# Two token blocks take turns over the halves of a layer's weights while those weights are still being split

## The chip, the core and the metric

The kernel runs on one core of a Trainium2 chip. Its engines are named as in the profile: PE (TensorE), DVE (VectorE), ACT (ScalarE), POOL (GpSimd) and SP (SyncE, which here only issues DMAs). The metric is the device time of one execution in microseconds. The kernel before takes 863.5 us (median of three runs, 862.19 to 864.65).

## What is computed

A linear attention with a decaying state, a two-layer network and a mixture of eight experts, all in float32:

```python
for t in range(S):                                   # B=4, H=8, S=768, D=48
    cur = einsum('bhd,bhe->bhde', u[None] * kt, vt)
    y[:, :, t] = einsum('bhd,bhde->bhe', rt, state + cur)
    state = wt[:, :, :, None] * state + einsum('bhd,bhe->bhde', kt, vt)
x = y as (3072, 384)
h = x @ w_in                                         # 384 -> 2048
x = (maximum(h, 0) + alpha * minimum(h, 0)) @ w_out  # 2048 -> 384
logits = x @ w_gate ; one expert of 8 for each token
out = gate * (maximum(x @ w1[e], 0) @ w2[e])
```

The part of `y` that comes from `u` is a diagonal term: for each token and head, c = sum over d of r*k*u, and then c*v.

## The kernel before

The 3072 tokens are 24 tiles of 128. Each tile goes through the attention (`att_tile`): a scan of the decays and its reciprocal on DVE (`scan`, `rec0`, `rec1`, `k`), r times the decays on POOL (`r`), scores on PE (`sc`), copied by ACT (`a0`, `a1`) and masked by POOL (`m0`, `m1`), the transposed k (`ktr` on PE, `ko` on ACT), the state (`kv`, `st`), the output on PE (`yst`, `yav0`, `yav1`), the sum with the diagonal term on DVE (`fin`), a transpose (`xtr`) and its split in a high and a low part (`xh` on ACT, `xl` on DVE). The diagonal term is made by two POOL products (`rk`: r*k, then *u), a sum over d on DVE (`c`) and a product with v (`cv`; on ACT for tiles 0 to 2, else on POOL).

Three tiles are a block of 384 tokens; there are eight. For each block the first layer pair runs in 16 steps, one for each 128 of the 2048 hidden columns. A step is nine matmuls of `p1` (three chunks of 384, each as high*high, high*low and low*high), an activation in three operations (ACT `gn`, DVE `gt`, then ACT `gh` and DVE `gl`, the split of the result) and, two steps later, nine matmuls of `p2` into three PSUM banks that hold the block's output. `p1` writes to two PSUM buffers and the splits have three, so PE can run some two steps ahead of DVE.

The weights arrive in 16 packed pieces, j = 0 to 15, even ones of w_in and odd ones of w_out. A piece is needed from hidden step j (an even j and the odd one behind it serve two steps). `wl_stages` unpacks each: ACT `rebase`, three operations of DVE (`words`), ACT `high`, and `low` on DVE for even j, on POOL for odd j. The raw words have two buffers, and so have the unpacked ones.

What sets the order: all steps are put into numbered slots, two for each step of PE; attention tiles, weight pieces and gates are hung on slots by the tables OPS, PRO_OPS and PRO_MOVED and by `s_tile`. Slots below zero are the prologue (tiles 0 to 2 and the first pieces) in a written order on all engines. From step 0 on the order on PE and POOL is as written, and a scheduler sets it on DVE, ACT and SP. Every engine works through its own list in order, so that an instruction that waits holds up all behind it.

When a block's 16 steps are done, `p2_out` copies its three banks into x2 (two by ACT, one by DVE), and `gate_block` makes the gate logits of the first six blocks on DVE: 24 products with a sum (`lv`, L492), four at a time over some 12 steps. After eight blocks follow the experts, in 16 units. `constants` (POOL, at the end of the prologue) makes index tables for the gates, and oma_s = 1 - alpha, which `gt` reads.

Of the kernel before, what the change touches and what calls it, by code (L numbers as in the profile page):

```python
# [99 lines left out]
def attention_mlp_moe(ctx, tc, dmaj, tmaj, ub, alpha, w_in, w_out, w_gate, w_gate_b, wexp, out):  # L100
# [23 lines left out]
    def load_tile(i):  # L124
        if i < NB:
# [11 lines left out]
        sp.dma_start(out=tm, in_=tmaj[i])  # L137
# [22 lines left out]
    ub_s = cst.tile([128, DM], F32, name="ub_s")  # L160
    al_s = cst.tile([128, NF1], F32, name="al_s")
# [106 lines left out]
    def att_tile(i, s0):  # L268
        cx = {}
        blk, j = divmod(i, NB)  # L270
        first, last = i % CPB == 0, i % CPB == CPB - 1
# [5 lines left out]
        def scan():  # L277
            dm = dm_t[i]
            ex = ap.tile([PR, NP, 129], F32, tag="ex", name="ex")
# [32 lines left out]
        def diag():  # L312
            tm = tm_t[i]
# [132 lines left out]
        def x_low():  # L446
# [162 lines left out]
    def p2(blk, f):  # L609
        if f == 0:  # L610
# [489 lines left out]
```

## Time and profile before

| | |
|---|---|
| median of the runs | 863.5 us |
| the profiled execution | 865.37 us, span 863.6 us, mean clock of PE 0.974 of full |
| busy over the span | PE 94%, DVE 74%, ACT 45%, POOL 35% |
| first matmul of step 0 (block 0) | 40.97 us |
| first of block 1, block 2, block 3 | 135.21, 202.73, 268.61 us |
| length of block 0, 1, 2 | 94.2, 67.5, 65.9 us |
| idle time of PE from 40 to 170 us that ended with something else's release | 23 us |

The starts of the blocks are found by counting the matmuls of L591 in the timeline of PE, nine for each step. The views used are: busy time by stretch, who waited for whom, groups of instructions by line and shape in a stretch, the DMA issues, and the timeline. Where durations of one engine overlap a little, an instruction begins some 0.08 us before the one ahead is recorded as ended.

### The profile page before, as it was taken

How to read it: one execution, taken by the hardware profiler on the slowest of the kernel's cores; microseconds unless marked ns; L12 is line 12 of the kernel's file. 1: busy time of each engine (PE TensorE's matmuls, PEld its weight loads, DVE VectorE, ACT ScalarE, POOL GpSimd, SP SyncE). 2: the span in 40 equal slices, each digit the busy share in tenths (PEclk: the TensorE clock that was granted, in tenths of full speed). 3: DMA queues.
4: the chain of work that ended last, by engine and by line, in shares of the span. 5: the costliest groups of instructions: out<-in, count | busy, mean ns of one | idle time of the engine just before them, and what ended most of it. 6: DMA issues, size and time to landing. Idle time of an engine off the chain costs nothing. (4 is left out here: it accounts for less than half of the span.)

```text
span 863.6 us, 14591 instructions
## 1 busy us (share of the span) xinstructions
PE 812.2 (94%) x5453; PEld 787.7 (91%) x5453; DVE 640.4 (74%) x1219; ACT 385.0 (45%) x751; POOL 298.4 (35%) x309
## 2 busy tenths in 40 slices
PE   6868779999999999999999999999899999999994
PEld 4767769999999999999999999989899999999993
DVE  6999997976967977976976973446766676767761
ACT  3555453343333334333334333346445566665641
POOL 5466654324433324334234341122423122322301
PEclk8788999999999999999999999999999999999998
DMA  9734543022324122322122300055367577686830
GB/s 277 213 107 149 200 147 122 29 60 87 60 60 117 32 60 66 83 60 84 63 61 60 88 1 1 28 201 211 120 235 250 195 237 282 228 288 194 287 104 21
DMA packets 30513, 111.59 MB, mean 129 GB/s; under 512 B 8229, under 2 KB 11592, under 8 KB 30440
## 3 DMA queue, kind: packets, MB, share of 16 engines
q1 hardware_dynamic: 26088, 100.38, 36.6%
q0 software_dynamic: 4352, 10.26, 3.3%
q8 instruction: 44, 0.72, 0.3%
q14 instruction: 29, 0.24, 0.1%
HBM read 100.95 MB, written 10.45 MB: 129 GB/s over the span
## 5 line engine op out<-in xcount | busy, mean ns | idle before, releaser
L591 PE MATMUL ph<-xth,wih 128*128 128x384 f32 x384 | 136.3, 355 | 11.1 <-DVE gt L596 9.0
L602 ACT CAST gh<-gt 128x384 fp32r<-128x384 f32 x128 | 65.6, 513 | 170.9 <-DVE gt L596 170.9
L617 PE MATMUL py<-woh,gh 128*128 128x384 f32 x384 | 136.6, 356 | 2.6 <-DVE x L628 1.3
L591 PE MATMUL ph<-xth,wil 128*128 128x384 f32 x384 | 131.0, 341 | 4.8 <-DVE wil L232 4.8
L591 PE MATMUL ph<-xtl,wih 128*128 128x384 f32 x384 | 130.9, 341 | 0.8 <-DVE xtl L449 0.8
L617 PE MATMUL py<-woh,gl 128*128 128x384 f32 x384 | 129.9, 338 | 0.0
L617 PE MATMUL py<-wol,gh 128*128 128x384 f32 x384 | 129.4, 337 | 0.0
L604 DVE TENSOR_TENSOR gl<-gt,gh 128x384 fp32r<-128x384 f32 x128 | 86.4, 675 | 32.9 <-ACT gh L602 31.3
L594 ACT ACTIVATE gn<-ph 128x384 f32<-128x384 f32 x128 | 62.5, 488 | 100.8 <-PE ph L591 97.1
L596 DVE SCALAR_TENSOR_TENSOR gt<-gn,oma_s,ph 128x384 f32<-128x384 f32 x128 | 76.4, 597 | 41.0 <-ACT gn L594 40.4
L492 DVE SCALAR_TENSOR_TENSOR sink<-x,wgb 128x384 f32<-128x384 f32 x144 | 98.8, 711 | 1.5 <-ACT x L628 1.2
L822 DVE SCALAR_TENSOR_TENSOR gl<-ph,gh 128x256 fp32r<-128x256 f32 x96 | 40.4, 422 | 74.0 <-ACT gh L820 73.7
L591 PEld LDWEIGHTS ph<-xth,wih 128*128 128x128 f32 x384 | 73.4, 191 | 13.2 <-DVE gt L596 9.9
L891 POOL DMA_INDIRECT out<-ys,meta x28 | 28.2, 1006 | 158.3 <-ACT ys L888 103.3
L817 PE MATMUL ph<-xh,w1h 128*128 128x256 f32 x288 | 81.1, 282 | 1.7 <-DVE gl L822 1.7
L817 PE MATMUL ph<-xh,w1l 128*128 128x256 f32 x288 | 80.8, 281 | 0.0
L817 PE MATMUL ph<-xl,w1h 128*128 128x256 f32 x288 | 80.3, 279 | 0.0
L591 PEld LDWEIGHTS ph<-xth,wil 128*128 128x128 f32 x384 | 73.2, 191 | 6.1 <-DVE wil L232 6.1
L617 PEld LDWEIGHTS py<-woh,gh 128*128 128x128 f32 x384 | 73.1, 190 | 5.2 <-DVE x L628 1.9
L363 POOL TENSOR_SCALAR_AFFINE_SELECT at<-at 128x512 f32<-128x512 f32 x46 | 37.2, 830 | 112.1 <-ACT at L359 112.1
L591 PEld LDWEIGHTS ph<-xtl,wih 128*128 128x128 f32 x384 | 73.5, 191 | 1.8 <-DVE xtl L449 1.6
L617 PEld LDWEIGHTS py<-woh,gl 128*128 128x128 f32 x384 | 72.8, 189 | 0.6 <-DVE gl L604 0.6
(211 smaller groups left out, 1939.2 us busy)
## 6 DMA issues: line engine op xcount, KB each, us to landing
raw<-w SPq DMA_DIRECT2D x64, 768.0 KB, 4.8
dm<-dmaj SPq DMA_DIRECT2D x21, 673.8 KB, 4.7
tm<-tmaj SPq DMA_DIRECT2D x21, 576.0 KB, 3.8
raw<-w_out SPq DMA_DIRECT2D x8, 768.0 KB, 4.4
raw<-w_in SPq DMA_DIRECT2D x7, 768.0 KB, 4.3
x2d<-x SPq DMA_DIRECT2D x8, 576.0 KB, 3.6
both<-tmaj SPq DMA_DIRECT2D x3, 576.0 KB, 9.1
wgb<-w_gate_b SPq DMA_DIRECT2D x2, 768.0 KB
```

What stands on the lines that cost most here:

```text
L363: pool.affine_select(out=cx[jj], in_=cx[jj], pattern=[[0, NP], [1, 128]], compare_op=ALU.is_gt, fill=0.0, base=0, channel_multiplier=-1,)
L492: vec.scalar_tensor_tensor(out=sink, in0=x2[:, j, :], scalar=1.0, in1=wgb_t[h][:, e, :], op0=ALU.mult, op1=ALU.mult, accum_out=cx["l"][:, ...
L591: pe.matmul(ph, lhsT=w, rhs=x[:, c, :], start=k == 0, stop=k == 3 * KC - 1)
L594: act.activation(gn, ph, AF.Relu, scale=-1.0)
L596: vec.scalar_tensor_tensor(out=gt, in0=gn, scalar=oma_s[:, f : f + 1], in1=ph, op0=ALU.mult, op1=ALU.add)
L602: act.copy(gh, gt)
L604: vec.tensor_tensor(out=gl, in0=gt, in1=gh.bitcast(F32), op=ALU.subtract)
L617: pe.matmul(y_t[blk][j], lhsT=g[:, sl], rhs=w, start=f == 0 and m == 0, stop=f == NF1 - 1 and m == 2,)
L817: pe.matmul(ph, lhsT=w, rhs=x, start=k == 0, stop=k == 3 * KC - 1)
L822: vec.scalar_tensor_tensor(out=gl, in0=ph, scalar=0.0, in1=gh.bitcast(F32), op0=ALU.max, op1=ALU.subtract)
L891: pool.indirect_dma_start(out=out, out_offset=bass.IndirectOffsetOnAxis(ap=d["meta"][:, j, 0:1], axis=0), in_=ys, in_offset=None, bounds_c ...
```

## The change

1. **Turns over the weights.** The steps of blocks 0 and 1 come in another order: block 0 with hidden steps 0 to 7, block 1 with 0 to 7, block 0 with 8 to 15, block 1 with 8 to 15. Weight pieces 8 to 15 move 16 slots (eight steps) back. The sums of one half are copied into x2 by `p2_out(half=True)`; after the second half DVE adds the banks to it (three additions).
2. **Tiles 3 to 8.** Block 1 now starts at step 8, so tiles 3, 4 and 5 stand at slots 0, 4 and 8, and tiles 6, 7, 8 at 38, 45 and 54 (`S_WAVE`), with tables PRE_OPS and POST_OPS that set their operations closer together. Before, tiles 3 to 5 were spread over 16 steps.
3. **The diagonal term of tiles 0 to 5** is one POOL product r*k in (d, t) layout; PE then sums over d with four small matmuls against u (two columns each), into spare columns of the bank of `ktr`; `ko` copies both. `rk` now stands ahead of `scan`. Only v of their third input array is loaded (192 of 576 KB), and the u table of 192 KB is loaded later.
4. **Tables.** The gates' index tables are made at slot 40. What stays at the prologue's end is one memset with two small DMAs, and oma_s, now on DVE.
5. `fin` writes onto cv; x has no buffer of its own any more, so `cv` of the next tile waits for the transpose of the one ahead.

The core of the diff:

```diff
+S_WAVE = (0, 4, 8, 38, 45, 54)
+PRE_OPS = {"scan": -5, "r": -5, "rec0": -4, "rec1": -3, "k": -2, "rk": -6}
@@ s_tile
+    if 0 < blk <= NWAVE:
+        return S_WAVE[i - NB]
@@ load_tile
-        sp.dma_start(out=tm, in_=tmaj[i])
+        sl = (slice(None), slice(2 if i < NCPE else 0, 3))
+        sp.dma_start(out=tm[sl], in_=tmaj[i][sl])
@@ fill / constants
+    def fill():
+        vec.tensor_scalar(oma_s, al_s, -1.0, 1.0, op0=ALU.mult, op1=ALU.add)
+        pool.memset(oobm, NT)
...
-        pool.tensor_scalar(oma_s, al_s, -1.0, 1.0, op0=ALU.mult, op1=ALU.add)
@@ diag
+            if i < NCPE:
+                rk = ap.tile([PR, NP, 128], F32, tag="x2b", name="rk", bufs=1)
+                pool.tensor_tensor(out=rk, in0=cx["r"], in1=cx["k"], op=ALU.mult)
+                cx["rk"] = rk
+                return
@@ ktr
+            if i < NCPE:
+                for p in range(NP):
+                    at = NP * PR + 2 * p
+                    pe.matmul(pa[:, at : at + 2], lhsT=cx["rk"][:, p, :], rhs=us_s[:, p, :], start=True, stop=True)
@@ fin
-            x = ap.tile([128, DM], F32, tag="x", name="x", bufs=1)
-            vec.tensor_tensor(out=x, in0=cx["y"], in1=cx["cv"].rearrange("p h d -> p (h d)"), op=ALU.add)
+            x = cx["cv"].rearrange("p h d -> p (h d)")
+            vec.tensor_tensor(out=x, in0=cx["y"], in1=x, op=ALU.add)
@@ p2_out
+            if blk < NWAVE and not half:
+                vec.tensor_tensor(out=x2[:, j, :], in0=y_t[blk][j], in1=x2[:, j, :], op=ALU.add)
@@ steps and pieces
-    msteps = [("m", b, f) for b in range(NBLK) for f in range(NF1)]
+    msteps = [("m", b, f + h) for h in (0, HALF) for b in range(NWAVE) for f in range(HALF)]
+    msteps += [("m", b, f) for b in range(NWAVE, NBLK) for f in range(NF1)]
-            s = [2 * j - WL_OFF + n for n in range(4)]
+            s = [2 * j - WL_OFF + n + (2 * HALF if j >= NWL // 2 else 0) for n in range(4)]
```

What this does to the engines' lists is shown at three places. POOL in the prologue, from the first tile's operations on; L295 is r, L315 and L316 are `rk`, L363 a mask. Before:

```order
L295 TENSOR_TENSOR both<-both,ex 112x512
L315 TENSOR_TENSOR rk<-both 128x384
L316 TENSOR_TENSOR rk<-rk,ub_s 128x384
L363 AFFINE_SELECT at_186<-at_186 128x512
L363 AFFINE_SELECT at_194<-at_194 128x512
```

Now (L341 is `rk`, L319 is r, L393 a mask):

```order
L341 TENSOR_TENSOR rk<-both 112x512
L319 TENSOR_TENSOR both<-both,ex 112x512
L341 TENSOR_TENSOR rk<-both 112x512
L393 AFFINE_SELECT at_185<-at_185 128x512
L393 AFFINE_SELECT at_199<-at_199 128x512
```

The `rk` of tiles 0 and 1 both stand ahead of the masks of tile 0, and each is one operation.

DVE around steps 1 and 2; L210, L211, L214 are the words of a weight piece, L232 its low part, L308 and L310 the tile's decays and k, L596 and L604 `gt` and `gl`, L397 the state. Before:

```order
L596 SCALAR_TENSOR_TENSOR gt<-gn,oma_s,ph 128x384
L214 SCALAR_TENSOR_TENSOR v_537<-raw,v_537 128x768
L604 TENSOR_TENSOR gl<-gt,gh 128x384
L596 SCALAR_TENSOR_TENSOR gt<-gn,oma_s,ph 128x384
L232 TENSOR_TENSOR wil_119<-v_537,wih_118 128x3x256
L210 TENSOR_SCALAR v_586<-v_586 128x768
L604 TENSOR_TENSOR gl<-gt,gh 128x384
```

Now (L641 and L649 are `gt` and `gl`, L334 is k, L435 the state, L306 the scan, L328 the reciprocal, L250 a low part):

```order
L334 TENSOR_TENSOR dm<-dm,rec 112x512
L641 SCALAR_TENSOR_TENSOR gt<-gn,oma_s,ph 128x384
L232 SCALAR_TENSOR_TENSOR v_561<-raw,v_561 128x768
L649 TENSOR_TENSOR gl<-gt,gh 128x384
L435 TENSOR_TENSOR st<-pv,st 112x384
L306 SCALAR_TENSOR_TENSOR ex<-both,apat 112x516
L641 SCALAR_TENSOR_TENSOR gt<-gn,oma_s,ph 128x384
L328 RECIPROCAL rec<-ex 112x128
L649 TENSOR_TENSOR gl<-gt,gh 128x384
L250 TENSOR_TENSOR wil_120<-v_561,wih_119 128x3x256
```

Between the same two `gt` stand now, beside the words of the weights, the state of tile 3 and the scan of tile 5; k of tile 4 is ahead of them.

DVE at the first steps of block 2 (now steps 34 and 35), where gates run; a sink is one of the 24 gate products, and the numbers behind lg and x2 name the block. Before, when block 2 had got to the same step, the sinks were all of one block:

```order
L492 SCALAR_TENSOR_TENSOR sink_2078,lg_2077<-x2_2046,wgb_1129 128x384
L596 SCALAR_TENSOR_TENSOR gt_2074<-gn_2072,oma_s_106,ph_2062 128x384
L492 SCALAR_TENSOR_TENSOR sink_2078,lg_2077<-x2_2046,wgb_1129 128x384
L492 SCALAR_TENSOR_TENSOR sink_2175,lg_2077<-x2_2046,wgb_1131 128x384
L604 TENSOR_TENSOR gl_2085<-gt_2074,gh_2083 128x384
```

Now:

```order
L641 SCALAR_TENSOR_TENSOR gt_2043<-gn_2041,oma_s_107,ph_2031 128x384
L537 SCALAR_TENSOR_TENSOR sink_2051,lg_2050<-x2_1250,wgb_1436 128x384
L537 SCALAR_TENSOR_TENSOR sink_2146,lg_1683<-x2_978,wgb_1438 128x384
L537 SCALAR_TENSOR_TENSOR sink_2051,lg_2050<-x2_1250,wgb_1436 128x384
L649 TENSOR_TENSOR gl_2058<-gt_2043,gh_2056 128x384
L537 SCALAR_TENSOR_TENSOR sink_2051,lg_2050<-x2_1250,wgb_1436 128x384
L435 TENSOR_TENSOR st_2101<-pv_2072,st_1848 112x384
L537 SCALAR_TENSOR_TENSOR sink_2146,lg_1683<-x2_978,wgb_1438 128x384
```

The sinks of block 0 (lg_1683) and block 1 (lg_2050) stand mixed in one stretch, five in a step.

## Rows read from the trace of the kernel before

**Rows 1.** Busy time by stretch: us, PE PEld DVE ACT POOL busy, PEclk, DMA, GB/s

```profile
41.00:88.00 47.00, 34.33 (x205) 32.42 (x203) 45.12 (x54) 26.06 (x50) 29.80 (x28) 0.85 0.38 132
88.00:135.20 47.20, 37.96 (x220) 35.62 (x221) 45.54 (x60) 21.25 (x38) 27.86 (x14) 0.93 0.51 174
135.20:202.70 67.50, 66.17 (x447) 64.37 (x447) 54.55 (x124) 25.42 (x60) 21.30 (x25) 1.00 0.21 67
202.70:268.60 65.90, 65.90 (x446) 64.28 (x446) 52.30 (x124) 23.44 (x55) 24.54 (x28) 1.00 0.26 68
```

**Rows 2.** Waits of PE, 40 to 170 us: us in total, times, longest

```profile
PE ph L591 <- DVE gt L596: 8.3, 2, 6.8
```

**Rows 3.** Groups of DVE by line, 41 to 135.2 us: count, busy us, mean ns

```profile
L210 DVE TENSOR_SCALAR v<-v 128x768 uint32<-128x768 uint32 x14 | 14.4, 1027 | 0.6 <-ACT v L206 0.6
L214 DVE SCALAR_TENSOR_TENSOR v<-raw,v 128x768 uint32<-128x768 uint32 x13 | 13.9, 1071 | 0.0
L211 DVE SCALAR_TENSOR_TENSOR v<-raw,v 128x768 uint32<-128x768 uint32 x13 | 12.2, 941 | 0.0
L604 DVE TENSOR_TENSOR gl<-gt,gh 128x384 fp32r<-128x384 f32 x15 | 11.6, 774 | 0.0
L232 DVE TENSOR_TENSOR wil<-v,wih 128x768 fp32r<-128x768 f32 x7 | 8.9, 1273 | 0.0
L308 DVE TENSOR_TENSOR rec<-rec,dm 112x128 f32<-112x128 f32 x9 | 8.5, 946 | 0.0
```

**Rows 4.** Timeline of DVE, single instructions: start us, us, what

```profile
42.80 3.32 DVE L210 TENSOR_SCALAR v<-v 128x768 uint32<-128x768 uint32 x1 [0.20 <-ACT v L206]
46.16 0.96 DVE L211 SCALAR_TENSOR_TENSOR v<-spare,v 128x768 uint32<-128x768 uint32 x1
...
56.03 0.39 DVE L308 TENSOR_TENSOR rec<-rec,dm 112x128 f32<-112x128 f32 x1
...
91.97 0.55 DVE L604 TENSOR_TENSOR gl<-gt,gh 128x384 fp32r<-128x384 f32 x1
...
93.31 0.55 DVE L210 TENSOR_SCALAR v<-v 128x768 uint32<-128x768 uint32 x1
```

**Rows 5.** Timeline of POOL: a low part, the first table, `rk` of a tile

```profile
43.76 1.81 POOL L232 TENSOR_TENSOR wol<-v,woh 128x768 fp32r<-128x768 f32 x1
45.51 0.20 POOL L248 MEMSET tri<- 128x128 bf16 x1
...
66.64 1.34 POOL L315 TENSOR_TENSOR rk<-tm 128x384 f32<-128x384 f32 x1
68.06 3.24 POOL L316 TENSOR_TENSOR rk<-rk,ub_s 128x384 f32<-128x384 f32 x1
```

**Rows 6.** Timeline of DVE in the prologue: scan and decays of tile 1, `c`

```profile
12.41 1.23 DVE L280 TENSOR_TENSOR_SCAN ex<-both,apat 112x516 f32<-112x516 f32 x1 [1.17 <-DMA both<-dmaj]
...
14.67 2.70 DVE L308 TENSOR_TENSOR rec<-rec,both 112x128 f32<-112x128 f32 x3
...
18.83 0.54 DVE L321 TENSOR_REDUCE c<-rk 128x8 f32<-128x384 f32 x1
```

**Rows 7.** DMA issues, 0 to 60 us: count, KB each, median us to landing

```profile
both<-tmaj SPq DMA_DIRECT2D x3, 576.0 KB, 9.1
```

**Rows 8.** Timeline of PE: scores of tile 2, first step, three 8-column products

```profile
26.20 1.83 PE L351 MATMUL pa<-both 48*128 48x128 f32 x16 [1.96 <-DVE both L310]
...
40.97 0.44 PE L591 MATMUL ph<-xth,wih 128*128 128x384 f32 x1
...
546.14 0.73 PE L481 MATMUL plg<-wg_s,x2t 128*128 128x8 f32 x6
```

**Rows 9.** Busy time of a stretch in the prologue, columns as in rows 1

```profile
28.00:30.00 2.00, 2.00 (x11) 2.00 (x11) 1.97 (x2) 1.95 (x6) 1.48 (x3) 0.50 1.00 269
```

**Rows 10.** Groups of DVE by line, 202.7 to 268.6 us, columns as in rows 3

```profile
L492 DVE SCALAR_TENSOR_TENSOR sink<-x,wgb 128x384 f32<-128x384 f32 x24 | 17.3, 744 | 0.3 <-ACT x L628 0.2
```

More of the change, by code (lines that the diff above doesn't have):

```diff
@@ L160, in attention_mlp_moe @@
     ub_s = cst.tile([128, DM], F32, name="ub_s")
+    us_s = cst.tile([PR, NP, 2], F32, name="us_s")
     al_s = cst.tile([128, NF1], F32, name="al_s")
@@ L270, in att_tile, with inputs @@
         blk, j = divmod(i, NB)
+        def inputs():
+            for n, at in (("r", 0), ("k", 512)):
+                cx[n] = dm_t[i][:, at : at + 512].rearrange("p (a t) -> p a t", a=NP)
         first, last = i % CPB == 0, i % CPB == CPB - 1
@@ L278, in scan @@
             dm = dm_t[i]
+            inputs()
             ex = ap.tile([PR, NP, 129], F32, tag="ex", name="ex")
@@ L373, in ktr @@
         def ktr():
-            pa = ps_a.tile([128, NP, PR], F32, tag="pa", name="pk")
-            for p in range(NP):
-                pe.transpose(pa[:, p, :], cx["k"][:, p, :], ident[:PR, :PR])
+            pa = ps_a.tile([128, NP * PR + H], F32, tag="pa", name="pk")
+            if not last:
+                for p in range(NP):
+                    pe.transpose(pa[:, PR * p : PR * p + PR], cx["k"][:, p, :], ident[:PR, :PR])
+            if i < NCPE:
+                for p in range(NP):
+                    at = NP * PR + 2 * p
+                    pe.matmul(pa[:, at : at + 2], lhsT=cx["rk"][:, p, :], rhs=us_s[:, p, :], start=True, stop=True)
             cx["pk"] = pa
         def ktr_out():
-            kt = ap.tile([128, NP, PR], F32, tag="kt", name="kt", bufs=1)
-            act.copy(kt, cx["pk"])
-            cx["kt"] = kt
+            kt = ap.tile([128, NP * PR + H], F32, tag="kt", name="kt", bufs=1)
+            sl = (slice(None), slice(NP * PR if last else 0, NP * PR + (H if i < NCPE else 0)))
+            act.copy(kt[sl], cx["pk"][sl])
+            cx["kt"] = kt[:, : NP * PR].rearrange("p (a d) -> p a d", a=NP)
+            if i < NCPE:
+                cx["c"] = kt[:, NP * PR :]
         def kv():
@@ L457, in att_tile @@
         if not last:
-            ops.update({"ktr": ktr, "ko": ktr_out, "pm": decay, "kv": kv, "st": state})
+            ops.update({"pm": decay, "kv": kv, "st": state})
+        for n in ("c",) if i < NCPE else ("ktr", "ko") if last else ():
+            del ops[n]
         for n, fn in ops.items():
@@ L620, in p2, with p2_out @@
                     rhs=w,
-                    start=f == 0 and m == 0,
-                    stop=f == NF1 - 1 and m == 2,
-                )
-    def p2_out(blk):
-        x2 = mp.tile([128, NB, DM], F32, tag="x2", name="x2", bufs=1)
-        for j in range(NB):
-            (vec.tensor_copy if j == 1 else act.copy)(x2[:, j, :], y_t[blk][j])
+                    start=h0 and m == 0,
+                    stop=h1 and m == 2,
+                )
+    x2_t = {}
+    def p2_out(blk, half=False):
+        if blk not in x2_t:
+            if half and blk:
+                x2_t[blk] = ap.tile([128, NB, DM], F32, tag="x2b", name="x2", bufs=1)
+            else:
+                x2_t[blk] = mp.tile([128, NB, DM], F32, tag="x2", name="x2", bufs=1)
+        x2 = x2_t[blk]
+        for j in range(NB):
+            if blk < NWAVE and not half:
+                vec.tensor_tensor(out=x2[:, j, :], in0=y_t[blk][j], in1=x2[:, j, :], op=ALU.add)
+            else:
+                (vec.tensor_copy if j == 1 else act.copy)(x2[:, j, :], y_t[blk][j])
+        if half:
+            return
         sp.dma_start(
@@ L1011, in attention_mlp_moe @@
             {"m": p2, "A": u_p2, "B": b_p2}[kind](b, f)
-            if kind == "m" and f == NF1 - 1:
+            if kind == "m" and f == HALF - 1 and b < NWAVE:
+                p2_out(b, half=True)
+            elif kind == "m" and f == NF1 - 1:
                 x2 = p2_out(b)
@@ L1074 @@
     ub = np.ascontiguousarray(np.broadcast_to(a["u"].reshape(1, DM), (128, DM)))
+    us = np.zeros((PR, NP, 2), np.float32)
+    for j in range(2):
+        us[64 * j : 64 * j + D, :, j] = a["u"].reshape(NP, 2, D)[:, j].T
     alpha = np.ascontiguousarray(a["moe_alpha"].reshape(NF1, 128).T)
```

48 lines of the change are left out of this document (32 added, 16 removed), and 8 rows, old and new, of tables (PRO_MOVED, PRO_OPS).

## The prediction

> **What bounds the kernel now.** I began with busy time by stretch. From block 2 on PE is busy all the time, 65.9 of 65.9 us, while DVE is busy 52.3 [rows 1]. Block 0, the first 16 steps from 41.0 to 135.2 us, is another matter: there DVE is busy 45.12 of 47.00 and 45.54 of 47.20 us, PE 34.33 and 37.96, and PE's clock is at 0.85 and 0.93 of full [rows 1]. So block 0 takes 94.2 us for work that PE does in 66, and DVE sets its pace. The second view, PE's waits, names DVE too: 8.3 us of waits for `gt`, the longest 6.8 [rows 2]. The third, DVE by line, shows why: the three word operations of a weight piece take 1.03, 1.07 and 0.94 us and the low part 1.27 [rows 3]; all but two of the 16 pieces fall in these 94 us. The most that the change could bring here is 94.2 + 67.5 - 2 x 66 = 30 us over blocks 0 and 1. The end follows one for one, since after block 1 PE is never free of work for long.
>
> **The important point of the order.** The weights of eight steps now serve sixteen, so half of the pieces could come after step 8. But in DVE's list as compiled they do not come much later: ahead of `gt` of step 14 (with it the PSUM buffer that step 16 needs comes free) stand the words of 13 pieces, where before 14 fell in block 0. Tiles 3, 4 and 5, spread over 16 steps before, stand in the first eight. The work of DVE over the first 16 steps is therefore nearly the same, and the gain must come from small terms.
>
> **The prologue (first step at 40.97 before).** The scan of tile 1 waits for its transfer until 12.41 [rows 6]. Ahead of it and with it in SP's queue are 226, 448, 576, 192 and 674 KB; 384 KB of the third-array load [rows 7] and the 192 KB table go or move. 576 of 2116 KB is at most 3.4 us of 12.4; part of that is start-up, and I take 2.3. Two sums `c` of 0.54 leave DVE ahead of the last tile [rows 6]: 1.1. The decays of tile 1 took 2.70 us for three [rows 6], against 0.39 for one that runs alone [rows 4], so 1.5 too much beside POOL; with one POOL product for two I give back half of this for each of tiles 1 and 2: 1.5. Against this, PE gets four products of two columns for each tile. Not one of these is in the trace. Bounds: nothing, if they run under waits; or what products of eight columns cost, 0.73 us for three [rows 8], so 1.0 for four, and double at the half clock that PE has here (0.50) [rows 9]. For tiles 0 and 1 PE has idle time ahead of the next scores (1.96 us ahead of tile 2's) [rows 8]; for tile 2 I take 1.0. Sum: 2.3 + 1.1 + 1.5 - 1.0 = 3.9 us earlier. Bounds: 1 us, if the one buffer of the new `rk` (the next product waits for PE's sums of the tile before) eats the earlier transfer, and 5.5, if PE has no idle time ahead of tile 2 and keeps its full clock.
>
> **Steps 0 to 15 (94.2 us before).** I count DVE's list from the end of the prologue to `gt` of step 14, before and now. One piece's words fewer: 1.03 + 1.07 + 0.94 = -3.0 [rows 3]. One low part: -1.3 [rows 3]. Three `c`: -1.6 [rows 6]. One `gt` and `gl`: about -1.3 (0.77 for `gl` [rows 3], 0.55 for `gt`, taken as `gl` alone [rows 4]). One more scan, reciprocal and decay operation, of tile 7: +1.2 [rows 6], +1.0 (not in the rows; between a decay and a scan) and +0.9 [rows 3], +3.1 in all. One copy of a half sum: +0.5, as `gl` alone [rows 4]. POOL: operations beside POOL are stretched, L210 1.03 for 0.55, L604 0.77 for 0.55, L308 0.95 for 0.39 [rows 3, 4]; times 14, 15 and 9 that is 6.7 + 3.4 + 5.0 = 15 us, for 57.7 us of POOL [rows 1], 0.26 for one. POOL loses one low part of 1.8 [rows 5] and some 2 us each for two tiles, whose pair (4.6 us in one instance [rows 5]) becomes one: 6 us, so -1.6. Waits: DVE was idle 94.2 - 90.7 = 3.5 us [rows 1]. I expect more, since the tiles follow each other at twice the pace; the mean wait of PE for `gt` was 8.3 / 2 = 4.2 [rows 2], and I take +2.5, less than one such. Sum: -3.0 - 1.3 - 1.6 - 1.3 + 3.1 + 0.5 - 1.6 + 2.5 = -2.7 us. PE's twelve small products of tiles 3 to 5 (3 us at full clock by the price above) lie under DVE here and cost nothing; without this cover they cost those 3 us.
>
> The gates' tables (POOL, from 45.51 on [rows 5]) I cost at nothing. The long L210 ahead of them, 3.32 us, had begun at 42.80 and was held by the low part that POOL ran until 45.57; L211 right after it, beside the tables, took 0.96 [rows 4, 5], as its mean of 0.94 [rows 3]. The Trainium skill says why (SBUF — State Buffer, section Who interferes with whom): an operation of DVE with two inputs in SBUF is held by one of GpSimd that reads SBUF, not by one that only writes, as memsets and index tables do. By that rule moving the tables gives nothing; counted like other POOL work their 2.7 us would give 0.7 more. The row agrees with the rule.
>
> **Steps 16 to 31 (67.5 us before).** DVE has little left of the weights, PE's steady 66 us are the bound. On top come block boundaries: the banks are now emptied four times in 32 steps instead of twice, the last times by three DVE additions that stand between `gt` and `gl`. PE waits for a bank for one or two DVE operations of some 0.55 us, 1 us each. I take 66 + 2 = 68: +0.5.
>
> **Steps 32 to 47 (65.9 before).** The gates of blocks 0 and 1 overlap, which they never did. In steps 24 to 40 stand 45 gate products instead of 24: 21 x 0.72 = 15.1 us (17.3 / 24) [rows 10]; with the additions, 18. DVE had 65.9 - 52.3 = 13.6 free in a block [rows 1]. The excess is 4.3 us, of which I let half vanish because tile work of block 2 is ahead by then: +2. Bounds 0 and 4.3. From there on the kernels agree: `fin` onto cv makes POOL wait for a transpose one slot later, beside masks that wait longer anyway.
>
> Together -3.9 - 2.7 + 0.5 + 2 = -4.1 us. The profiled execution took 865.4 us (span 863.6), so it would be 861.3; on the median of the runs, 863.5, I predict **859.4 us**.
>
> **Rivals.** *The gain is larger.* For: DVE's idle time does not grow, PE meets no idle time ahead of tile 2 and runs the prologue at full clock instead of 0.50 [rows 9], the gates fit in, banks cost nothing: 2.5 + 1.5 + 2 + 2 more, -12.1, 851.4 us. Against: this needs four lucky ends at once, and DVE's list is as long as I counted it.
>
> *Nothing comes of it.* DVE's work over the two blocks is only moved; it was busy 145 of 161.7 us [rows 1] and stays at that. With the prologue at its lower bound (+2.9) and the gates at theirs (+2.3) it gives +1.1, 864.6 us.
>
> *Slower: three tiles in eight steps wait for each other.* The scores, states and outputs of a tile share three PSUM buffers. In PE's new list the scores of tile 4 stand ahead of `p2` of step 0 and `p1` of step 3, and they need the bank that is free only after `fin` of tile 3; on DVE that `fin` stands behind the words of two pieces and the low part shown in the change. `gt` of step 3 then waits for the scores and 18 matmuls, with DVE holding little in between. The same holds for tiles 4 and 5, and once more where block 1 waits for the low part of tile 5. Three waits of the mean size, 4.2 [rows 2], are 12.5 in place of my 2.5: +10, so +5.9, 869.4 us. For it: PE's clock falls after such waits (0.85 here), which lengthens each. Against: DVE's list holds some four operations in each gap. It decides from 6.6 us of waits on: there the whole gain is gone.
>
> **How the numbers follow.** Forecast 0.38, with its own range 855 to 861; the larger gain 0.22; nothing 0.18; slower 0.22. About 0.3%, 2.6 us, is what a measurement of this kernel can tell from no change. Faster by more than that: 0.38 + 0.22 = 0.60; same 0.18; slower 0.22. For 8 in 10 the range reaches to both outer cases: 848 to 870.
>
> **What would show it.** Right if the first step starts at 36 to 38 us, step 16 near 128 (was 135.2), step 32 near 196 (was 202.7), and the 16 steps from there take 67 to 69 us; if DVE is above 93% busy over the first 16 steps; and if the tables' move shows in no DVE duration. The larger gain is shown by step 16 before 122. The slower case is shown by waits of PE for `fin`, or of DVE for `gn`, of over 6.6 us between steps 2 and 9, with step 16 after 135. Wrong in the whole if the experts, which I take as unchanged, take another time from their first matmul on.

## The result and the profile after

The changed kernel took 875.02 us (median of four runs, 871.59 to 880.48) beside 864.07 (862.19 to 864.65) before: a ratio of 1.0118, 95% interval 1.0079 to 1.0157. The forecast was 4 us less; it became 11 more. The profiled execution took 872.84 us, span 871.1, which is 7.5 more than the span of before.

The page of the kernel after, its first lines:

```profile
span 871.1 us, 14699 instructions
PE 823.2 (94%) x5501; PEld 797.7 (92%) x5501; DVE 643.8 (74%) x1220; ACT 385.9 (44%) x752; POOL 290.6 (33%) x302
```

Nothing there tells where the 7.5 us are. The start of every step does, found as before by counting nine matmuls of `p1` (now L636) for each. All kernels of this study, one profiled execution each, in us:

| kernel | first step | steps 0-7 | steps 0-15 | steps 16-31 | steps 32-47 |
|---|---|---|---|---|---|
| before | 40.97 | 45.4 | 94.2 | 67.5 | 65.9 |
| after | 41.16 | 63.3 | 91.2 | 72.1 | 71.7 |
| after_again | 47.13 | 62.8 | 90.7 | 72.5 | 72.7 |
| turns_old_diag | 41.52 | 63.3 | 92.1 | 72.8 | 70.7 |
| diag_no_turns | 50.52 | 45.7 | 90.0 | 71.1 | 65.8 |
| one_block_order | 42.67 | 45.8 | 90.9 | 70.9 | 65.8 |
| gate1_later | 47.01 | 63.4 | 91.2 | 71.2 | 72.3 |
| masks_together | 46.63 | 58.5 | 86.4 | 72.5 | 72.6 |
| warm24 | 41.90 | 62.1 | 90.0 | 72.1 | 71.6 |
| two_rk | 47.41 | 57.5 | 85.6 | 72.7 | 71.9 |
| no_fillers | 47.95 | 61.8 | 89.7 | 72.1 | 71.3 |
| gates_short | 41.07 | 62.8 | 90.4 | 68.5 | 66.0 |
| tiles_earlier | 50.29 | 63.4 | 91.9 | 79.3 | 76.2 |
| masks_and_warm | 42.90 | 56.6 | 84.5 | 72.6 | 73.1 |
| all_three | 43.81 | 57.5 | 85.3 | 68.5 | 66.1 |

From step 48 to the end every kernel takes the same within 3 us (594.9 to 597.8; steps 64 to 111 alone take 198.0 to 198.2 in all of them). So in the profiled execution the loss lies ahead of step 48: the prologue gave nothing, the first 16 steps gave the forecast 3 us, and the next 32 cost 10.4.

Busy time of after by stretch, the answer to [rows 1]; columns as there. The stretches are steps 0 to 7, 8 to 15, 16 to 23 and so on:

```profile
41.16:104.44 63.28, 51.13 (x306) 48.98 (x304) 57.88 (x71) 30.58 (x60) 30.81 (x21) 0.78 0.34 119
104.44:132.32 27.88, 25.82 (x146) 24.86 (x146) 27.72 (x38) 15.05 (x27) 10.67 (x7) 1.00 0.35 117
132.32:166.37 34.05, 32.23 (x212) 30.47 (x212) 25.17 (x39) 16.04 (x34) 12.88 (x20) 1.00 0.31 105
166.37:204.42 38.05, 34.64 (x236) 33.88 (x235) 31.56 (x73) 11.79 (x28) 15.59 (x13) 1.00 0.27 84
204.42:240.82 36.40, 32.80 (x222) 31.40 (x222) 32.80 (x88) 12.58 (x28) 12.33 (x14) 1.00 0.16 52
240.82:276.15 35.33, 35.10 (x226) 34.35 (x225) 25.73 (x59) 10.66 (x26) 14.44 (x19) 0.95 0.37 74
```

PE, busy for 66.17 and 65.90 us of blocks 1 and 2 before [rows 1], now has gaps: 3.4 us of 38.05, 3.6 of 36.40. Its largest waits, in steps 0 to 15 (the answer to [rows 2]), 16 to 31 and 32 to 47 (us in total, times, longest):

```profile
PE pv L426 <- ACT kt L417: 4.6, 1, 4.6
PE py L455 <- POOL at L393: 4.2, 1, 4.2
PE pk L411 <- DVE xtl L487: 2.5, 1, 2.5
```

```profile
PE px L476 <- DVE cv L465: 3.4, 1, 3.4
PE py L664 <- ACT x L685: 1.6, 1, 1.6
```

```profile
PE prk L580 <- POOL g_ac L569: 2.2, 1, 2.2
PE ph L636 <- DVE xtl L487: 1.4, 1, 1.4
```

The waits of 8.3 us for `gt` [rows 2] are down to 0.4; others have come, each at one tile or one gate.

**The prologue.** Single instructions of DVE: decays of tile 0, scan and decays of tile 1.

```profile
5.92 2.49 DVE L332 TENSOR_TENSOR rec<-rec,both 112x128 f32<-112x128 f32 x3
...
9.94 1.23 DVE L306 TENSOR_TENSOR_SCAN ex<-both,apat 112x516 f32<-112x516 f32 x1 [0.74 <-DMA both<-dmaj]
...
12.20 1.23 DVE L332 TENSOR_TENSOR rec<-rec,both 112x128 f32<-112x128 f32 x3
```

The smaller loads bring the scan of tile 1 forward by 2.47 us (12.41 before [rows 6]), and its decays take 1.23 instead of 2.70. But this does not get through. POOL and PE in the same execution:

```profile
13.51 1.26 POOL L341 TENSOR_TENSOR rk<-both 112x512 f32<-112x512 f32 x1 [5.76 <-PE pk L411]
14.73 1.22 POOL L393 TENSOR_SCALAR_AFFINE_SELECT at<-at 128x512 f32<-128x512 f32 x2
```

```profile
9.30 1.67 PE L381 MATMUL pa<-both 48*128 48x128 f32 x16 [2.30 <-issue]
...
11.70 1.73 PE L411 MATMUL pk<-us_s,rk 112*128 112x2 f32 x8
...
25.45 1.16 PE L381 MATMUL pa<-both 48*128 48x128 f32 x16 [1.46 <-DVE both L334]
```

POOL's second `rk` waits 5.76 us until PE has summed the first, the masks of tile 0 stand behind it, and PE runs its first products below full clock (scores in 1.67 us, where 1.16 is full clock). From 9.30 to 20 us PE has no idle time: its own list is what the scores of tile 1 wait for, where before it stood idle for 3.05 us until DVE was ready:

```profile
18.69 1.22 PE L351 MATMUL pa<-both 48*128 48x128 f32 x16 [3.05 <-DVE both L310]
```

Tile 2's scores start 0.75 us earlier than before (26.20 [rows 8]), the first step 0.2 later.

**Steps 31 and 32.** DVE's list ahead of the block boundary; a sink is a gate product, `cv` (L465) is the sum of tile 8, for which PE's transpose waits 3.4 us (the rows of 0.08 us that read an accumulator are left out):

```profile
195.04 1.35 DVE L649 TENSOR_TENSOR gl<-gt,gh 128x384 fp32r<-128x384 f32 x1
196.31 1.37 DVE L537 SCALAR_TENSOR_TENSOR sink<-x,wgb 128x384 f32<-128x384 f32 x1
...
198.59 0.55 DVE L351 TENSOR_REDUCE c<-rk 128x8 f32<-128x384 f32 x1 [0.90 <-POOL rk L346]
199.06 0.55 DVE L537 SCALAR_TENSOR_TENSOR sink<-x,wgb 128x384 f32<-128x384 f32 x1
...
200.85 0.56 DVE L537 SCALAR_TENSOR_TENSOR sink<-x,wgb 128x384 f32<-128x384 f32 x1
...
201.33 0.61 DVE L641 SCALAR_TENSOR_TENSOR gt<-gn,oma_s,ph 128x384 f32<-128x384 f32 x1
201.86 0.55 DVE L465 TENSOR_TENSOR cv<-py,cv 128x384 f32<-128x384 f32 x1
```

Between `gl` of one step and `gt` of the next there are five gate products and a sum `c` that waits for POOL: 5 us without anything that PE needs. PE had finished the outputs of tile 8 at 195.85 us; DVE came to `cv` at 201.86.

**Step 39.** The largest wait behind step 32, 2.2 us, is for the end of the gate of block 0 itself. PE's product `prk`, which ranks its tokens, needs POOL's running sum `g_ac`. POOL comes to it only behind the masks of a tile and its r; the masks wait for ACT's copy `at`, which stands in ACT's list behind `gh` and so behind a `gt` (234.26 us) that DVE makes between gate products. POOL, PE, and a stretch of 2 us right after (columns as in [rows 1]):

```profile
235.97 1.61 POOL L393 TENSOR_SCALAR_AFFINE_SELECT at<-at 128x512 f32<-128x512 f32 x2 [7.24 <-ACT at L389]
...
239.28 2.24 POOL L569 TENSOR_TENSOR g_ac<-g_ac,g_oh 128x8 bf16<-128x8 bf16 x3
```

```profile
240.80 0.17 PE L580 MATMUL prk<-g_ac,ones 128*128 128x24 bf16 x1 [2.20 <-POOL g_ac L569]
```

```profile
242.00:244.00 2.00, 2.00 (x10) 1.98 (x10) 1.46 (x5) 1.00 (x2) 1.92 (x2) 0.50 0.00 0
```

The two waits of 2.2 and 1.4 us are nearly all of the loss of steps 32 to 39 (36.40 us instead of 32.57). Steps 40 to 47 (35.33 instead of 33.31) have no such wait, but the granted clock is at 0.50 from 242 to 244 us and at 0.67 to 246.

### The profile page after: what moved, and what is told of

It is laid out like the page before. It is cut to its first block, busy times and chain, and to the rows that moved or that the text cites. A ratio compares the mean times of both kernels' runs of the same rounds, so it can differ in the third digit from the quotient of the medians.

```text
span 871.1 us, 14699 instructions
## 1 busy us (share of the span) xinstructions
PE 823.2 (94%) x5501; PEld 797.7 (92%) x5501; DVE 643.8 (74%) x1220; ACT 385.9 (44%) x752; POOL 290.6 (33%) x302
## 5 line engine op out<-in xcount | busy, mean ns | idle before, releaser
L664 PE MATMUL py<-woh,gh 128*128 128x384 f32 x384 | 136.8, 356 | 3.5 <-ACT x L685 1.6
L636 PE MATMUL ph<-xth,wih 128*128 128x384 f32 x384 | 135.1, 352 | 1.4 <-DVE gt L641 1.3
L636 PE MATMUL ph<-xtl,wih 128*128 128x384 f32 x384 | 130.1, 339 | 2.9 <-DVE xtl L487 2.9
L636 PE MATMUL ph<-xth,wil 128*128 128x384 f32 x384 | 129.7, 338 | 0.0
L649 DVE TENSOR_TENSOR gl<-gt,gh 128x384 fp32r<-128x384 f32 x128 | 94.3, 737 | 36.6 <-ACT gh L647 35.0
L641 DVE SCALAR_TENSOR_TENSOR gt<-gn,oma_s,ph 128x384 f32<-128x384 f32 x128 | 76.5, 597 | 40.4 <-ACT gn L639 39.7
L537 DVE SCALAR_TENSOR_TENSOR sink<-x,wgb 128x384 f32<-128x384 f32 x144 | 93.8, 671 | 1.3 <-ACT x L685 0.9
L636 PEld LDWEIGHTS ph<-xth,wih 128*128 128x128 f32 x384 | 72.8, 190 | 6.0 <-DVE gt L641 2.6
L636 PEld LDWEIGHTS ph<-xtl,wih 128*128 128x128 f32 x384 | 72.8, 190 | 4.5 <-DVE xtl L487 4.5
L664 PEld LDWEIGHTS py<-woh,gl 128*128 128x128 f32 x384 | 73.1, 190 | 1.0 <-DVE gl L649 1.0
L664 PEld LDWEIGHTS py<-wol,gh 128*128 128x128 f32 x384 | 73.3, 191 | 0.0
L636 PEld LDWEIGHTS ph<-xth,wil 128*128 128x128 f32 x384 | 72.6, 189 | 0.0
```

The costliest lines, as they stand in the source:

```text
L537: vec.scalar_tensor_tensor(out=sink, in0=x2[:, j, :], scalar=1.0, in1=wgb_t[h][:, e, :], op0=ALU.mult, op1=ALU.mult, accum_out=cx["l"][:, ...
L636: pe.matmul(ph, lhsT=w, rhs=x[:, c, :], start=k == 0, stop=k == 3 * KC - 1)
L641: vec.scalar_tensor_tensor(out=gt, in0=gn, scalar=oma_s[:, f : f + 1], in1=ph, op0=ALU.mult, op1=ALU.add)
L649: vec.tensor_tensor(out=gl, in0=gt, in1=gh.bitcast(F32), op=ALU.subtract)
L664: pe.matmul(y_t[blk][j], lhsT=g[:, sl], rhs=w, start=h0 and m == 0, stop=h1 and m == 2,)
```

## The experiments

**Which part costs it: the turns or the diagonal term?** turns_old_diag keeps the turns and takes the diagonal term back to two POOL products and a sum on DVE:

```diff
-NCPE = NB * NWAVE
+NCPE = 0
```

(with the prologue slots of `rk` and `cv` of before, and ub loaded first).

> The changed kernel with the diagonal term of all tiles as it was before (two POOL products, the sum on DVE, the full third-array load, the prologue's rk at its old places); the turns over the weights' halves and the late tables stay. Theory 1 (the turns cost the time: overlap of two gates, three tiles in eight steps): first step at 41 us, steps 16 to 47 still take 142 to 144 us against 133 in the kernel before, in all 870 to 876 us. Rival (PE's small sums of the diagonal term and their one buffer cost it): steps 0 to 15 shorter by 3 us or more than in the changed kernel, in all at or below 866 us.

Measured: 875.87 us (875.39 to 877.72), ratio 1.0112 (1.0085 to 1.0140); steps 16 to 47 took 143.5 us. diag_no_turns is the reverse, the change without the turns (in this kernel r*k of tiles 4 and 5 is made from an r already decayed, so their diagonal term is off; the instructions are the same):

```diff
-NWAVE = 2
+NWAVE = 0
...
-NCPE = NB * NWAVE
+NCPE = 2 * NB
```

(The loads and weight pieces go back to their old slots too.)

> The changed kernel with the turns taken out: blocks one after the other, weight pieces, tiles and loads at the places of the kernel before; the new diagonal term of tiles 0 to 5, fin onto cv and the late tables stay. Theory 1: 860 to 865 us, within 0.4% of the kernel before, steps 16 to 47 back at 133 us. Rival: 868 us or more. In both the first step is at 41 us, if the one buffer of rk eats the earlier scan of tile 1.

Measured: 873.2 us (866.34 to 876.03), ratio 1.0063 (1.0033 to 1.0093); steps 32 to 47 back at 65.8 us, but steps 16 to 31 at 71.1 and the first step at 50.52. So neither expectation fits: steps 16 to 47 took 136.8 us, 7 less than with the turns and 3.4 more than before. The turns cost most of the time behind step 16, not all of it, and the new diagonal term seems to do something to the prologue, where the kernel with the old one started its first step at 41.

**Is it the overlap of two gates?** gate1_later hangs the gate of block 1 ten slots later:

```diff
-                end = gate_block(b, x2, 2 * i + 1)
+                end = gate_block(b, x2, 2 * i + 1 + (10 if b == 1 else 0))
```

> The changed kernel with the gate of block 1 started ten slots (five steps) later, so that it lies between those of blocks 0 and 2. If the overlap of two gates is what steps 32 to 47 lost: these 16 steps take 67 to 69 us instead of 71.7, in all 870 to 872 us. If not (the loss is in the waits for tiles): 71 us as before and 874 to 876.

Measured: 880.09 us (879.48 to 881.33), ratio 1.0155 (1.0128 to 1.0183); steps 16 to 47 in 143.5 us, as without the edit. The gates of the two blocks had overlapped by four products only, since the scheduler places them on DVE; now they don't at all, and nothing is gained. The overlap that the prediction priced is not the cause.

**The waits in step 1.** In after POOL comes to the second mask of tile 3 only behind two products for tile 4 (`rk` and r) and the `cv` of its own:

```profile
54.33 0.67 POOL L393 TENSOR_SCALAR_AFFINE_SELECT at<-at 128x512 f32<-128x512 f32 x1 [7.79 <-ACT at L389]
54.97 1.86 POOL L341 TENSOR_TENSOR rk<-dm 112x512 f32<-112x512 f32 x1
56.91 2.06 POOL L319 TENSOR_TENSOR dm<-dm,ex 112x512 f32<-112x512 f32 x1
58.94 0.82 POOL L361 TENSOR_TENSOR cv<-tm,kt 128x384 f32<-128x384 f32 x1
59.72 1.09 POOL L393 TENSOR_SCALAR_AFFINE_SELECT at<-at 128x512 f32<-128x512 f32 x1
```

```diff
-    "ktr": 0, "a0": 0, "m0": 0, "a1": 0, "m1": 1, "ko": 1, ...
+    "ktr": 0, "a0": 0, "m0": 0, "a1": 0, "m1": 0, "ko": 1, ...
```

> The changed kernel with the second mask of tiles 3 to 5 one slot earlier on POOL, ahead of the next tile's rk and r. PE waited 4.2 us for it in step 1 and ran at half clock behind that. If PE's waits set steps 0 to 8: step 8 comes 4 to 8 us earlier than 104.5, in all 867 to 871. If DVE's work sets them: step 8 within 2 us of 104.5, in all 873 to 876.

Measured: 874.08 us (871.02 to 877.80), ratio 1.0078 (1.0049 to 1.0107). Steps 0 to 7 took 58.5 us, 4.8 less, and of PE's wait of 4.2 us for the mask 0.6 is left. In this execution the first step started at 46.63, though nothing was changed in the prologue.

**Is the prologue unsteady?** The changed kernel again, unaltered:

> The changed kernel once more, unaltered, to see how far its prologue differs from one execution to the next. In its first profiled execution the first step of the blocks started at 41.16 us, in two kernels with the same prologue at 46.63 and 47.01. Theory 'the new prologue is unsteady': the profiled execution again starts its first step anywhere from 41 to 50 us, whatever its length the steps from there to the end of step 47 take 234 to 236 us (235.0 before), and the runs spread over 5 us or more while those of the kernel before spread over less than 7. Rival 'the late starts belong to the other two kernels': first step at 41.2 within 0.5, profiled execution 872 to 873.5.

Measured: 878.99 us (874.19 to 882.30), ratio 1.0111 (1.0056 to 1.0167); first step at 47.13, from there to the end of step 47 235.8 us. The theory holds. How far the prologue of the kernel before varies is not known: its runs spread too (862.19 to 871.24 us over all sets), and only one execution of it is in a trace. PE in this one:

```profile
9.33 2.08 PE L381 MATMUL pa<-both 48*128 48x128 f32 x16 [1.85 <-issue]
...
17.07 3.54 PE L455 MATMUL py<-both,at 128*128 128x48 f32 x16
...
21.50 2.08 PE L381 MATMUL pa<-both 48*128 48x128 f32 x16
...
29.14 1.16 PE L381 MATMUL pa<-both 48*128 48x128 f32 x16 [0.97 <-POOL both L319]
```

Scores that take 1.16 us at full clock take 2.08, until 25 us. The late execution of gate1_later shows the granted clock for it (12 to 20 and 20 to 30 us: PE busy 8.00 of 8.00 and 10.00 of 10.00, clock 0.50, the lower of the two levels):

```profile
12.00:20.00 8.00, 8.00 (x38) 7.14 (x38) 1.60 (x4) 3.72 (x14) 3.59 (x4) 0.50 1.03 330
20.00:30.00 10.00, 10.00 (x52) 7.84 (x51) 4.53 (x7) 4.43 (x15) 3.32 (x3) 0.50 0.68 212
```

**Buffer, clock or fillers?** Three edits of the prologue. two_rk gives `rk` two buffers, warm24 puts eight more warm-up products ahead of PE's first scores, no_fillers takes the warm-up products between the tiles out.

```diff
-                rk = ap.tile([PR, NP, 128], F32, tag="x2b", name="rk", bufs=1)
+                rk = ap.tile([PR, NP, 128], F32, tag="rk" if i % 2 else "x2b", name="rk", bufs=1)
```

> The changed kernel with two buffers that take turns for rk (the odd tiles use the buffer that the later tiles' rk has). Theory 'one buffer of rk': the waits of GpSimd for TensorE's sums (5.76 and 4.77 us, up to 9.2 in late executions) go, the masks of tile 0 no longer stand behind such a wait and come at about 12 us instead of 14.73, the first step starts 2 to 4 us earlier than the 41.16 of the changed kernel, at 37 to 39, and late starts of 46 to 50 do not appear. Theory 'the clock': the waits go, but TensorE remains at half clock, its products fill the time, and the first step stays at 41 or later, up to 47.

Measured: 875.88 us (875.66 to 878.14), ratio 1.0099 (1.0061 to 1.0137); first step at 47.41. POOL no longer waits for PE (second and third `rk` at 10.18 and 14.86, the masks at 12.39), but PE is at clock 0.50 from 12 to 30 us and the scores of tile 2 come at 30.36. So in a prologue at half clock the buffer's waits cost nothing: PE's own list was late anyway. What they cost in an early one no run shows. Behind the prologue the second buffer does gain: steps 0 to 7 took 57.5 us instead of 63.3; PE's wait for `pk` (2.5 us in after) is not there; the wait for the second mask is, with up to 3.7 us.

```diff
-WARM0 = 16
+WARM0 = 24
```

> The changed kernel with 24 instead of 16 warm-up products, 8 more of 0.30 us each (4.83 us for 16), so that TensorE has work until its first scores at about 9.3 us instead of standing idle for 2.30 us. Theory 'the clock': TensorE falls to half clock in that idle time, the sixteen score products then take 1.67 to 2.08 us instead of 1.16, and the rest of the prologue inherits it. Expected by it: scores of tile 0 in 1.16 us, those of tile 1 as well, first step at 37 to 39 us in this execution, the whole at 868 to 870. Theory 'one buffer of rk': the clock changes little, GpSimd's second and third product r*k still wait 4 us and more each for TensorE's sums of the tile ahead, first step at 40.5 to 41.5 at best.

Measured: 873.47 us (870.63 to 875.63, ten runs), ratio 1.0065 (1.0043 to 1.0087). PE:

```profile
9.81 1.16 PE L381 MATMUL pa<-both 48*128 48x128 f32 x16 [1.79 <-issue]
...
17.41 1.16 PE L381 MATMUL pa<-both 48*128 48x128 f32 x16
...
23.94 1.16 PE L381 MATMUL pa<-both 48*128 48x128 f32 x16 [1.51 <-DVE both L334]
...
28.10 3.54 PE L455 MATMUL py<-both,spare 128*128 128x48 f32 x16
...
35.30 3.54 PE L455 MATMUL py<-both,at 128*128 128x48 f32 x16
```

As the theory of the clock has it, all three groups of scores take 1.16 us, and those of tile 2 start 2.26 us earlier than before [rows 8]: the gain of the smaller loads is there. Then the clock falls all the same (granted 0.63 from 25 to 30 us, 0.50 from 30 to 40), the outputs of tiles 1 and 2 take 3.54 each, and the first step is at 41.90, not at 37 to 39. So this was half right: the clock decides, but the edit holds it for two thirds of the prologue only.

```diff
-PRO_WARM = ((9.6, 6), (11.5, 3), (14.8, 4), (15.65, 3), (21.55, 4), (22, 5))
+PRO_WARM = ((21.55, 4), (22, 5))
```

> The changed kernel without the four groups of warm-up products between the tiles of the prologue (6, 3, 4 and 3 products; the first 16 and the last 9 stay). Theory 'TensorE's own list sets the prologue': in the late executions TensorE is busy 8.00 of 8.00 us from 12 to 20 us and 10.00 of 10.00 from 20 to 30, at half clock, and the fillers stand in that list with 2.08 + 1.16 + 1.44 + 1.17 = 5.85 us. Without them the scores of tile 2 start at 24 to 26 us in every execution (25.45 in the early one, 29.14 and 30.36 in late ones), the first step at 40 to 43, and the runs spread less. Rival 'the fillers keep the clock up': the clock stays at half throughout, and the first step is at 44 or later.

Measured: 879.99 us (878.90 to 881.58), ratio 1.0162 (1.0134 to 1.0191). The rival holds: all scores take 2.08 us, those of tile 2 start at 27.95, the first step at 47.95. Without the fillers no run was below 878.90 us, while the eight runs of the changed kernel go from 871.59 to 882.30: taking them out gained nothing.

**Is it the gate products at all?** gates_short makes those of blocks 0 and 1 short:

```diff
+            w = 48 if blk < NWAVE else DM
-                    out=sink,
-                    in0=x2[:, j, :],
+                    out=sink[:, :w],
+                    in0=x2[:, j, :w],
...
-                    in1=wgb_t[h][:, e, :],
+                    in1=wgb_t[h][:, e, :w],
```

> The changed kernel with the gate products of blocks 0 and 1 over 48 of the 384 columns only (the other columns are left out of the gate's sums; all else is as it is), which takes some 0.4 of the 0.7 us off each of the 48. Looked at for steps 16 to 47 alone, 143.8 us in the changed kernel and 133.4 before. Theory 'the gates bunch': with them short VectorE is no longer full (it was busy 10.0 of 10.0 us from 220 to 240) and the 32 steps take 133 to 136 us. Rival 'the tiles and block ends wait for each other': the gates had spare time to run in, the waits for cv, xtl and the bank (3.4, 1.4 and 1.6 us in steps 31 to 33) stay, and the 32 steps take 140 or more.

Measured: steps 16 to 47 in 134.5 us (863.95 in one run); PE waits for nobody from step 24 to step 47. The three stretches of eight steps from step 24 on:

```profile
165.55:199.96 34.41, 34.41 (x235) 33.93 (x235) 24.83 (x75) 12.07 (x29) 12.46 (x13) 1.00 0.30 93
199.96:232.67 32.71, 32.63 (x222) 31.31 (x222) 24.92 (x109) 12.54 (x29) 10.04 (x15) 1.00 0.18 58
232.67:266.00 33.33, 33.33 (x227) 32.73 (x227) 19.16 (x35) 10.64 (x25) 12.59 (x18) 1.00 0.40 78
```

So 9.3 of the 10.4 us hang on the 48 gate products. They are as many as before the change, when PE's one wait from step 16 to 47 was 1.3 us for a bank. The wait of 1.6 us for a bank in steps 16 to 23 is still there.

**Amount or place?**

```diff
-S_WAVE = (0, 4, 8, 38, 45, 54)
+S_WAVE = (0, 4, 8, 28, 37, 46)
```

> The changed kernel with tiles 6, 7, 8 at slots 28, 37 and 46 instead of 38, 45 and 54, so that tile 8 is done before the gate products of block 0 begin (slot 49). Looked at for steps 16 to 47. Theory 'place': the gates cost only where an operation that TensorE waits for (cv and xtl of tile 8, waits of 3.4 and 1.4 us) stands behind gate products in VectorE's list. Steps 24 to 31 then take 34 to 35.5 us instead of 38.0, steps 32 to 47 stay at 71 to 72. Rival 'amount': VectorE has too much to do in steps 24 to 47 whatever the order; the 32 steps stay at 142 to 144 us.

Measured: 896.29 us (one run), steps 16 to 47 in 155.5; a miss for both theories as they stand. Steps 16 to 23 took 50.3 us: a tile's load now waits 25.8 us in SP's queue for its buffer, and the weights' loads behind it. But the eight steps after that show what was asked:

```profile
SPq L152 <- PE py L443: 25.8, 1, 25.8
```

```profile
192.47:221.44 28.97, 28.97 (x182) 28.93 (x181) 24.54 (x63) 9.51 (x21) 6.05 (x5) 1.00 0.21 66
```

With tile 8 finished, PE is busy for 28.97 of 28.97 us while DVE makes 20 gate products in that stretch, as many as in after. That fits the place in front of tile 8's `cv` as what costs in steps 24 to 31; it does not prove it, since the tile's own work has left the stretch as well (DVE busy 24.54 us instead of 31.56). For steps 32 to 47 this run decides nothing.

**Without the turns, mended.** one_block_order is diag_no_turns with 24 warm-up products and `rk` of tiles 4 and 5 in its right place:

```diff
+                o = ... -10 if n == "rk" and i < NCPE else OPS[n]
```

> The changed kernel without the turns (steps, pieces and tiles 3 to 8 in the old order) and with 24 warm-up products at the start; the diagonal term by r*k and TensorE, the smaller loads, the tables and the target of the tile's sum stay as in the changed kernel, with r*k of tiles 4 and 5 ahead of r's decay. Theory 'the turns cost 10 us in steps 16 to 47, the new diagonal term gains up to 4 us in steps 0 to 15': first step at 41 to 43, steps 0 to 15 in 90 to 91.5 us (94.2 in the kernel before), steps 16 to 47 in 133.5 to 135, in all 1 to 3 us less than the kernel before. Rival 'the diagonal term's small products cost TensorE as much as they save VectorE': steps 0 to 15 in 94 to 95, in all 1 to 4 us more than the kernel before.

Measured: 868.85 us (865.72 to 872.88, twelve runs), ratio 1.0024 (1.0002 to 1.0047). Steps 0 to 15 took 90.9 us, 3.3 less than before, as the theory says; steps 16 to 31 gave it back (70.9 instead of 67.5, where PE waits 2.3 us for a bank at the end of block 0 and its clock falls to 0.85), so that the rest of the theory missed. From the first step to step 48 it is 227.6 us, the same as before. What is left of the change without the turns is worth nothing, and the prologue 1.7 us late makes the difference. In steps 16 to 47 this kernel takes 3.3 us more than the one before, and the turns add 7.1 to that.

**Do the three places add up?** masks_and_warm joins masks_together and warm24; all_three adds the short gates.

> The changed kernel with 24 warm-up products at the start and the second mask of tiles 3 to 5 right behind the first: both edits that gained something alone. If the two losses are separate and add up, the first step starts at 42 us (41.9 with the warm-up alone), steps 0 to 7 take 57 to 58.5 us (58.5 with the masks alone, 63.3 without), steps 16 to 47 stay at 143 to 145, and the whole is 868 to 870 us, still 3 to 5 above the kernel before. If they are one loss seen twice (the wait for the mask is long only because TensorE comes early, or the low clock moves elsewhere), steps 0 to 7 take over 61 us or the time comes back by step 16, and the whole stays at 872 to 874.

Measured: 869.04 us (866.47 to 873.01, twelve runs), ratio 1.0014 (0.9993 to 1.0034): not told apart from the kernel before. First step at 42.90, steps 0 to 7 in 56.6, steps 16 to 47 in 145.7, 0.7 above the range.

> The same with the gate products of blocks 0 and 1 over 48 of 384 columns (the other columns are left out of the gate's sums). If prologue, mask and gates are the whole of the loss, the three gains add up: first step at 42, steps 0 to 7 in 57 to 58.5, steps 16 to 47 in 134 to 135, the whole at 858 to 861 us, below the kernel before and where the forecast of the change lay. If something else costs time as well, it stays above 862.

Measured: 860.68 us (858.48 to 862.99), ratio 0.9930 (0.9896 to 0.9964), 6.2 us below the kernel before. First step at 43.81, later than expected; the rest in its ranges. The three places are separate, and together they are the difference. The short gates leave out work that the kernel before does, so this run says where the time goes and is no repair: no kernel with the full computation beat the one before.

## Why the prediction was wrong, step by step

The profiled execution was forecast at 861.3 us and took 872.8. Of these 11.5 us some 4 lie in the prologue, 4 in steps 16 to 31 and 4 in steps 32 to 47.

**Prologue: forecast -3.9, measured +0.2 in one execution and +6 in the next.** The terms for DVE were right or low: 2.3 for the transfer (2.47), 1.5 for the decays (1.5 for tile 1 alone), though the first `rk`, now ahead of r, stretched the decays of tile 0 to 2.49 us (1.52 before) and brought its scores to 9.30 (8.32 before). The step that failed is the 1.0 for PE. I took PE's idle time ahead of the scores as cover for the four small products, and counted the same time as the gain of an earlier DVE. Before, PE stood idle 3.05 us ahead of the scores of tile 1 and 1.96 ahead of those of tile 2, 5.0 in all. The products of tiles 0 and 1, 1.9 us at full clock and 3.5 at half, come out of these 5.0; so by my estimate from these rows the scores of tile 2 could come 3.1 or 1.5 us earlier at most (0.75 in after, 2.26 in warm24), and tile 2's own products take 1.0 or 1.7 of that.

The price of the products was right: 1.73 us a tile at half clock and 0.96 at full, by the bounds 2.0 and 1.0. In the late executions the clock adds to it: at half clock from its first scores on, PE has no idle time until 28 us in after_again, and its list sets the prologue. The lower bound blamed the one buffer of `rk`; two_rk shows that in such an execution it costs nothing. The upper bound, 5.5, has no sum behind it: 3.9 with the 1.0 given back is 4.9.

**Steps 0 to 15: forecast -2.7, measured -3.0 (-3.5 in after_again).** Right in size, in part by luck. In after DVE is busy 85.6 us instead of 90.7, 5.1 less (forecast 5.2), and idle 5.6 instead of 3.5 (forecast +2.5). But in after_again it is busy 81.8 and idle 8.8 us (90% busy, where my sign was above 93), and the stretch is as long; in masks_together it is busy 81.3 and the stretch takes 86.4. The same work of DVE in 4.3 us less: its list alone does not set the length, as I had it. The slower rival's mechanism, tiles that wait for each other, was in there: PE waited 4.6 and 4.2 us in step 1, and 2.5 for `pk` later, 11.3 in all where the rival had 12.5. But it was ACT's copy of kt and POOL's second mask that PE waited for first, not `fin`; beside them DVE worked on, and step 16 came at 132.3 us, not after 135.

**Steps 16 to 31: forecast +0.5, measured +4.6.** I named block boundaries (the wait of 1.6 us for ACT's copy is one) and took DVE as free. The gate of block 0 runs here, 20 products in the last eight steps; I had counted them only against DVE's free time in steps 32 to 47.

**Steps 32 to 47: forecast +2, bounds 0 to 4.3, measured +5.8.** The mechanism was the gates, but my reckoning was one of capacity: so much work against so much free time of DVE. gate1_later took the overlap away and gained nothing; gates_short shows that nearly all of it is the gates. In steps 24 to 31 DVE is not even full (31.56 of 38.05 us), and from 220 to 240 us it is (19.98 of 20). In both, what PE needs stands behind the products in lists that are worked through in order: `cv` and `xtl` of tile 8, then the gate's own `prk`, 3.4 + 1.4 + 2.2 us. The clock that falls behind the last one accounts for most of the 2 us of steps 40 to 47. I had no term for either. The two gates overlapped by four products only, so the +2 had the right sign for the wrong reason.

**Tables: costed at nothing, right as far as DVE's rows show.** No run has them back in their old place. The long word operation beside POOL's state product and low part is still there without them. DVE and POOL of after:

```profile
43.59 3.41 DVE L229 SCALAR_TENSOR_TENSOR v<-spare,v 128x768 uint32<-128x768 uint32 x1
```

```profile
43.05 1.37 POOL L436 TENSOR_TENSOR st<-st,pm 112x384 f32<-112x384 f32 x1 [8.90 <-ACT v L224]
44.38 1.80 POOL L250 TENSOR_TENSOR wol<-v,woh 128x768 fp32r<-128x768 f32 x1
```

The row agrees with the rule that the prediction took from the Trainium skill (SBUF — State Buffer, Who interferes with whom): the operation, which has two inputs, did not end (47.00) until POOL's operations with inputs in SBUF were done (46.18). The prediction used the rule for L210 too, which has only one input; of its 3.32 us the rule as quoted says nothing, and only L211's 0.96 beside the tables bears it out there.

**Experts taken as unchanged: right**, 273.6 us from their first matmul to the end against 273.7, and 198.2 us for steps 64 to 111 against 198.1.

Left open: why the clock falls in one execution and not in the next (it fell after 1.85 us of idle time in after_again and held after 1.79 in warm24); how the gates' cost in steps 32 to 47 divides between their order and DVE being full (busy 32.80 of 36.40); and what two buffers for `rk`, the earlier mask and the longer warm-up give together, which no run joins.

## What to carry to other kernels

Work that fits into an engine's free time still costs when its list is in order and the work stands ahead of something that another engine waits for; look at what is late next at that place, here the last tile ahead of a block, before counting free microseconds. Idle time that an earlier operand is to remove cannot also cover new work: count it once. The same list of PE at the other clock has a different length, and a forecast of a prologue needs both. Where the start of a stage differs by 6 us between executions of one kernel, compare stages from their own start and not only whole times.

## What was not expected of the hardware

Four float32 products with two columns took 0.96 us at full clock, 0.24 each, and 1.73 at half; three with eight columns took 0.73 [rows 8], 0.24 each as well. So the number of columns made no difference here. All of PE's float32 groups in the prologue show the two levels plainly: scores 1.16 and 2.08 us, outputs 1.91 and 3.54, sums 0.96 and 1.73. In after_again and no_fillers the granted clock in the prologue's rows reads 1.00 while the same products take 2.08; there the durations were believed.
